# Loading q and k in runs of four tokens instead of two in a fused attention and SiLU kernel

## The chip, the core and the metric

The kernel runs on one core of a Trainium2 chip. The core has a matrix engine (TensorE, PE in the profile), a vector engine (VectorE, DVE), an activation engine (ScalarE, ACT), a general engine (GpSimd, POOL) and a queue engine (SyncE, SP) that here only issues transfers. Sixteen DMA engines move data between the device memory and the on-chip memory; each engine of the core works through its own instruction list in order and waits on semaphores for what others produce. The metric is the time of one execution in microseconds; lower is better.

## The reference

Eight batches with eight heads of attention over 576 tokens of 64 dimensions, with a decay made from the gates `f`, then a two-layer network with a SiLU on all 4,608 tokens:

```python
scores = scale * np.matmul(q, k.transpose(0, 1, 3, 2))
log_f = np.log(np.clip(f, 0.0001, 1.0))
cum = np.cumsum(log_f, axis=-1)
decay = cum[:, :, :, None] - cum[:, :, None, :]
scores = np.where(causal, -1000000000.0, scores + decay)
attn = softmax(scores)                  # over the last axis
x = (attn @ v) as [B * S, H * D]        # 4608 x 512
h = x @ w_in                            # 512 -> 2048
out = (h * sigmoid(h)) @ w_out          # 2048 -> 512
```

## The kernel before

**Pairs and tiles.** The 64 heads are worked in 16 groups of four (n = 0 to 15, two to a batch; below also called pairs, since q and k of a group share a tile). A group's q and k lie in one staging tile `stg` (two buffers): partition 32 j + t belongs to head j of the group and to token t of every run of tokens. `load_qk` issues one DMA for each head and tensor. Its access pattern takes the sequence in blocks of R x T tokens (T = 32): partition t gets R tokens that follow one another, so one contiguous piece has R x 64 floats. With R = 2 a piece has 512 bytes, a block has 64 tokens, and the 576 tokens are G = 9 blocks.

**From load to product.** `cast_qk` (mostly on GpSimd) turns fp32 in `stg` into bf16 in `raw`. `transposes` runs one VectorE transpose of 32 x 32 blocks over `raw` and writes `qkT`, in which a token is a column; because a partition holds R neighbouring tokens, neighbouring values of a transposed row go to columns R apart. TensorE then forms scores (`chunk`, line 350), ScalarE takes the exponential (line 360), GpSimd masks the diagonal blocks (line 387) and scales v by the decay (line 263), TensorE multiplies by v (line 429), and VectorE writes the normalised result to `xT` (line 457). The network follows on blocks of 512 tokens: `m1_chunk` (matrix product line 482, tanh line 490, gate line 493) and `m2_part` (product line 516, copy line 526, store line 527).

**The order.** Nothing is scheduled by a planner. The string `ORDER` lists the steps, each step adds its instructions to the engines' lists, and each engine follows its own list. The steps that the change and the prediction speak of:

- `G n.i` (lines 109 and 562): load the second part of group n's q (i = 0) or k (i = 1) on SyncE's queue, for n = 0 and 1 alone. The first part, blocks 0 to GA - 1 (256 tokens), is loaded ahead of the list. `L n.i`: the whole tensor, for n from 2.
- `y`, `c`, `C`: the casts of the first part, second part and the whole (line 136). `z`, `t`, `T`: the transposes of the same (line 279).
- `I i`, `O i`: a quarter of the first or second weight, issued by GpSimd on the software queue with a cast on the way (lines 190 and 199). `W`, `V`: load and scale a piece of v (lines 144 and 263).
- `S n.c`, `s i`: scores. `H`: half of a network step for the first 512 tokens, `A`: a whole one, `B`: a quarter of the second product.

On GpSimd the beginning of the list is: c0.0, c0.1, I0, two pieces of v, I1, one piece of v, c1.0, c1.1, I2, I3, C2.1, C2.0, O2. On SyncE it is: first parts, two pieces of v, G0.0, G0.1, two pieces of v, G1.1, G1.0, L2.1, a piece of v, L2.0, and on. Each DMA on the hardware queues waits on a semaphore for the one issued eight places before it.

Of the kernel before, what the change touches and what calls it, by code (L numbers as in the profile page):

```python
# [52 lines left out]
def kernel(  # L53
# [10 lines left out]
    nc = tc.nc  # L64

    B, H, S, D = q.shape
# [5 lines left out]
    QH = 4  # L72
# [3 lines left out]
    ST = S - SM  # L76
    NM = SM // P
    T = 32
    R = 2
    G = S // (R * T)  # L80
    E = R * D
    assert D == 64 and S == 576 and DM == H * D and H == QB * QH
    scale = 1.0 / float(D) ** 0.5
# [19 lines left out]
    vst: dict[int, list] = {}  # L103


    def qk_tile(n):
        return qkp.tile([P, 2, S * D // T], BF16, name="raw", tag="raw")

    def load_qk(n, i, engs, g0=0, g1=G, heads=(0, 2, 1, 3)):
        b, g = divmod(n, QB)  # L110
        direct = engs == (nc.gpsimd,)
        where = raw if direct else stg
        if n not in where:
            if direct:
                where[n] = qk_tile(n)
            else:
                where[n] = stage.tile([P, 2, S * D // T], FP32, name="stg", tag="stg", bufs=2)
        src = (q, k)[i]
        for j in heads:
            engs[j * len(engs) // QH].dma_start(  # L120
                out=where[n][j * T : (j + 1) * T, i, g0 * E : g1 * E].rearrange(
                    "p (g e) -> p g e", e=E
                ),
                in_=src[b, QH * g + j, g0 * R * T : g1 * R * T, :].rearrange(
                    "(g t c) d -> t g (c d)", t=T, c=R
                ),
            )

    def cast_qk(n, i, g0=0, g1=G, eng=nc.gpsimd):
        if n not in raw:  # L130
            raw[n] = qk_tile(n)
        r = slice(g0 * E, g1 * E)
        if eng is nc.scalar:
            eng.copy(out=raw[n][:, i, r], in_=stg[n][:, i, r])
        else:
            eng.tensor_copy(out=raw[n][:, i, r], in_=stg[n][:, i, r])  # L136
# [9 lines left out]
            in_=v[b, :, c * P : min(S, (c + 1) * P), :].rearrange("h p d -> p h d"),  # L146
        )

    GA = 4
    both = (nc.sync, nc.scalar)  # L150
    f_sb = setup.tile([BH, S], FP32, name="f_sb")
    nc.sync.dma_start(out=f_sb[:, :], in_=f.rearrange("b h s -> (b h) s"))
    for i in (1, 0):
        load_qk(0, i, both, 0, GA)
    load_qk(1, 0, (nc.sync,), 0, GA)
    nc.scalar.preload_act_table_set("natural_log_exp_and_others")
    for c in range(2):
# [10 lines left out]
        out=neg[:, :],  # L168
        in_=neg[:, :],
# [11 lines left out]
    for t in vps:  # L181
        nc.gpsimd.memset(t[0:ST, NM, :, :, :], 0.0)
    load_qk(1, 1, (nc.gpsimd,), 0, GA)

    WQ = 4
# [83 lines left out]

    def transposes(n, i, g0=0, g1=G):  # L270
        if n not in qkT:
            t = qktp.tile([P, 4 * S], BF16, name="qkT", tag="qkT")

            w = (0, GA * R * T, S) if n < QB else (0, S)
            qkT[n] = {
                w0: t[:, 4 * w0 : 4 * w1].rearrange("p (i x c) -> p i x c", i=2, x=2)
                for w0, w1 in zip(w, w[1:])
            }
        nc.vector.transpose(  # L279
            out=qkT[n][g0 * R * T][:, i, :, :].rearrange(  # L280
                "p x (g t c) -> p g c x t", t=T, c=R
            ),
            in_=raw[n][:, i, g0 * E : g1 * E].rearrange(
                "p (g c x e) -> p g c x e", c=R, x=2, e=T
            ),
        )

    def qk_cols(n, r, i, x, c0, w):
        o = max(o for o in qkT[n] if o <= c0)
# [262 lines left out]
    def nums(n):  # L552
# [5 lines left out]
        "u": decay_sum,  # L558
        "w": decay_weights,
        "y": lambda n, i: cast_qk(n, i, 0, GA, start_cast.get((n, i), nc.gpsimd)),  # L560
        "z": lambda n, i: transposes(n, i, 0, GA),
        "G": lambda n, i: load_qk(n, i, (nc.sync,), GA, G),
        "f": lambda n: products([(n, None)], 0, HB, "log"),
# [4 lines left out]
        "o": lambda i: gate(w_out_bf[0:1, (i + 1) * NFC // WQ - 1, 0:1], WQ + i),  # L568
        "L": lambda n, i: load_qk(n, i, (nc.sync,)),
        "c": lambda n, i: cast_qk(n, i, GA, G),  # L570
        "t": lambda n, i: transposes(n, i, GA, G),
        "C": cast_qk,
        "T": transposes,
        "W": load_v,
        "V": convert_v,
# [51 lines left out]
```

## Time and profile before

| what | value |
|---|---|
| runs | 353.04 and 351.63 us, median 352.34 |
| the profiled execution | 352.01 us, of which the span is 350.3 |
| PE busy | 323.5 us, 92% of the span |
| DVE busy | 222.8 us, 64% |
| ACT busy | 209.4 us, 60% |
| POOL busy | 129.1 us, 37% |
| DMA packets | 86416, 42.54 MB; 41128 of them under 512 B |
| DMA issues for q and k on SyncE | 136, median 0.45 us each |
| transposes of q and k on VectorE | 36, 46.4 us busy |

The span runs from the first to the last instruction; the execution's own time also has what lies around it. The busy share is a mean over the whole span. The page also cuts the span into 40 slices and gives each engine's busy share there in tenths (9 is 90% or more), and follows a chain of waits backward from the last instruction: at each step to what released it. TensorE's granted clock is full in nearly all of it (0.998).

### The profile page before, as it was taken

The numbers are of one execution on the slowest core, as the hardware profiler recorded it, in microseconds if no ns is written. First come the engines' busy times: TensorE is split into PE (matmuls) and PEld (weight loads), VectorE is DVE, ScalarE is ACT, GpSimd is POOL, SyncE is SP. The second block draws the span as 40 slices with busy tenths as digits, with TensorE's granted clock in tenths as the row PEclk, the third lists the DMA queues.
The fourth block names the chain that finished last, engine by engine and source line by source line (L and its number), as shares of the span: only waits on it lengthen the run. The fifth ranks groups of instructions, "written<-read, shape, count | busy, mean of one in ns | idle before, by whom it ended". The sixth has DMA issues, their size and how long they took to land.

```text
span 350.3 us, 8957 instructions
## 1 busy us (share of the span) xinstructions
PE 323.5 (92%) x3739; PEld 165.6 (47%) x3782; DVE 222.8 (64%) x297; ACT 209.4 (60%) x298; POOL 129.1 (37%) x172
## 2 busy tenths in 40 slices
PE   1667789999999999999999999999999999999996
PEld 1454554544455445444554455454445444444444
DVE  4466875688958696679867677679566834334310
ACT  3585796469854984599539855766574344444421
POOL 7771828628484362245543654322150000000000
PEclk9999999999999999999999999999999999999999
DMA  7999999898679803951299142223100000010102
GB/s 169 201 219 221 217 213 197 245 232 190 152 164 233 190 3 109 251 140 31 63 241 225 32 123 80 60 62 92 47 30 32 32 30 33 31 60 31 61 30 90
DMA packets 86416, 42.54 MB, mean 121 GB/s; under 512 B 41128, under 2 KB 81832, under 8 KB 86376
## 3 DMA queue, kind: packets, MB, share of 16 engines
q1 hardware_dynamic: 80936, 37.39, 43.7%
q0 software_dynamic: 4864, 4.33, 8.0%
q8 instruction: 29, 0.48, 0.6%
q10 hardware_dynamic: 576, 0.26, 0.3%
q14 instruction: 11, 0.09, 0.1%
HBM read 36.85 MB, written 9.44 MB: 132 GB/s over the span
## 4 chain that ended last, share of the span: by engine, by line
PE 79%; DMA 8%; ACT 4%; DVE 3%; issue 3%; POOL 2%; SPq 1%; ACTq 0%; POOLq 0%
PE po L516 34%; PE hp L482 30%; PE ps L429 9%; PE sc L350 6%; DMA w_in_bf<-in_moe_w_in_dram 3%; ACT u L360 2%; DMA stg<-in_k_dram 2%; DVE gt L493 2%; DMA vf<-in_v_dram 1%; ACT th L490 1%; POOL w_in_bf L190 1%; DMA f_sb<-in_f_dram 1%; POOL vp L263 1%; SPq L120 0%; POOL raw L136 0%
## 5 line engine op out<-in xcount | busy, mean ns | idle before, releaser
L493 DVE SCALAR_TENSOR_TENSOR gt<-th,hp 128x512 bf16<-128x512 bf16 (+1 forms) x160 | 96.1, 627 | 74.7 <-ACT th L490 74.0
L482 PE MATMUL hp<-xT,w_in_bf 128*128 128x512 bf16 (+1 forms) x622 | 135.7, 358 | 4.0 <-DMA w_in_bf<-in_moe_w_in_dram 3.0
L516 PE MATMUL po<-w_out_bf,gt 128*128 128x512 bf16 (+1 forms) x567 | 130.8, 373 | 3.1 <-issue 2.7
L490 ACT ACTIVATE th<-hp 128x512 bf16<-128x512 f32 (+1 forms) x160 | 83.8, 560 | 39.8 <-PE hp L482 37.6
L360 ACT ACTIVATE u<-sc 128x2048 bf16<-128x2048 f32 (+7 forms) x64 | 95.0, 1503 | 20.7 <-PE sc L350 20.6
L482 PEld LDWEIGHTS <-w_in_bf 128*128 128x128 bf16 x640 | 59.4, 98 | 66.4 <-issue 5.6
L516 PEld LDWEIGHTS <-gt 128*128 128x128 bf16 x592 | 55.3, 98 | 63.8 <-issue 2.8
L387 POOL TENSOR_SCALAR_AFFINE_SELECT u<-u 128x512 bf16<-128x512 bf16 (+1 forms) x70 | 40.0, 591 | 86.8 <-ACT u L360 86.3
L468 DVE RECIPROCAL rec<-rec 128x144 f32<-128x144 f32 x56 | 55.6, 1023 | 3.8 <-ACT rec L448 3.8
L279 DVE STREAM_TRANSPOSE qkT<-raw 128x1152 bf16<-128x1152 bf16 (+2 forms) x36 | 46.4, 1308 | 6.0 <-POOL raw L136 5.9
L263 POOL TENSOR_TENSOR vp<-vf,w_bf 128x512 bf16<-128x512 f32 (+1 forms) x40 | 41.4, 1041 | 18.3 <-DMA vf<-in_v_dram 17.4
L136 POOL CAST raw<-stg 128x1152 bf16<-128x1152 f32 (+2 forms) x34 | 36.2, 1075 | 28.4 <-DMA stg<-in_q_dram 24.2
L526 ACT ACTIVATE osb<-po 128x512 f32<-128x512 f32 (+1 forms) x37 | 21.7, 588 | 29.8 <-PE po L516 28.7
L350 PE MATMUL sc<-qkT 32*128 32x64 bf16 (+7 forms) x1064 | 32.4, 249 | 4.9 <-ACT u L360 2.9
L448 ACT ACTIVATE rec<-ps 128x192 f32<-128x192 f32 (+1 forms) x28 | 10.0, 408 | 43.4 <-DVE xT L457 43.1
L457 DVE TENSOR_TENSOR xT<-ps,rec 128x512 bf16<-128x512 f32 (+1 forms) x28 | 19.9, 753 | 16.2 <-PE ps L429 16.0
L350 PEld LDWEIGHTS <-qkT 32*128 32x128 bf16 x1064 | 17.6, 95 | 25.3 <-issue 20.3
L429 PEld LDWEIGHTS <-vp 128*32 128x32 bf16 x960 | 20.4, 98 | 3.9 <-issue 1.0
L429 PE MATMUL ps<-u,vp 128*32 128x320 bf16 (+4 forms) x784 | 21.6, 261 | 0.1
L429 PEld LDWEIGHTS <-w_bf 128*32 128x32 bf16 x480 | 9.2, 96 | 11.9 <-issue 8.1
L429 PE MATMUL ps<-u,w_bf 128*32 128x192 bf16 (+2 forms) x392 | 12.2, 263 | 0.1
L251 PE MATMUL wps<-ident_f,wexp 64*128 64x64 f32 x5 | 0.8, 316 | 7.6 <-ACT wexp L244 7.6
(37 smaller groups left out, 47.5 us busy)
## 6 DMA issues: line engine op xcount, KB each, us to landing
out_dram<-osb SPq DMA_DIRECT2D x35, 256.0 KB, 2.4
vf<-in_v_dram SPq DMA_DIRECT2D x32, 256.0 KB, 4.3
stg<-in_k_dram SPq DMA_DIRECT2D x56, 144.0 KB, 4.4
stg<-in_q_dram SPq DMA_DIRECT2D x56, 144.0 KB, 4.0
w_in_bf<-in_moe_w_in_dram POOLq DMA_DIRECT2D x8, 256.0 KB, 7.9
w_out_bf<-in_moe_w_out_dram POOLq DMA_DIRECT2D x4, 512.0 KB, 10.5
vf<-in_v_dram SPq DMA_DIRECT2D x8, 128.0 KB, 4.6
stg<-in_q_dram SPq DMA_DIRECT2D x8, 80.0 KB, 4.8
```

The source lines that it names most:

```text
L136: eng.tensor_copy(out=raw[n][:, i, r], in_=stg[n][:, i, r])
L263: nc.gpsimd.tensor_tensor(out=vp[r, c, :, :, :], in0=vst[b][c][r, :, :].rearrange("p h (r x) -> p h x r", x=2), in1=w_bf[r, c, b * H : (b ...
L279: nc.vector.transpose(out=qkT[n][g0 * R * T][:, i, :, :].rearrange("p x (g t c) -> p g c x t", t=T, c=R), in_=raw[n][:, i, g0 * E : g1 * E ...
L350: nc.tensor.matmul(sc[:, j, o : o + w], lhsT=qk_cols(n, r, 1, x, k_off(kb), P), rhs=qk_cols(n, r, 0, x, q0, w), start=(x == 0 and not unde ...
L360: nc.scalar.activation(out=us[n][:, :, c0:c1], in_=sc[:, :, at : at + c1 - c0], func=ACT.Exp, scale=scale,)
L387: nc.gpsimd.affine_select(out=x, in_=x, pattern=[[0, QH], [1, w]], compare_op=ALU.is_ge, fill=0.0, base=0 if kb < NM else ST, channel_mult ...
L429: nc.tensor.matmul(ps[32 * j : 32 * j + 32, o0 + q0 - e0 : o0 + q1 - e0], lhsT=w, rhs=us[n][:, j, o : o + q1 - q0], start=(kb == 0), stop= ...
L468: nc.vector.reciprocal(out=recs[n][:, r], in_=recs[n][:, r])
L482: nc.tensor.matmul(hp[:, 0 : hi - lo], lhsT=w_in_bf[:, cc, fc * P : (fc + 1) * P], rhs=xT[:, cc, t0 + lo : t0 + hi], start=(cc == 0), stop ...
L490: nc.scalar.activation(out=th[:, 0 : hi - lo], in_=hp[:, 0 : hi - lo], func=ACT.Tanh, scale=0.5)
L493: nc.vector.scalar_tensor_tensor(out=gt[:, fc, lo:hi], in0=th[:, 0 : hi - lo], scalar=1.0, in1=hp[:, 0 : hi - lo], op0=ALU.add, op1=ALU.mult,)
L516: nc.tensor.matmul(po[:, 0 : c1 - c0], lhsT=gt[:, fc, tb * P : (tb + 1) * P], rhs=w_out_bf[:, fc, c0:c1], start=(fc == 0), stop=(fc == NFC ...
```

## The change

R goes from 2 to 4, so a contiguous piece has four tokens or 1 KB, and a block 128 tokens. 576 tokens are four such blocks and 64 tokens more; this rest keeps the old form of two tokens (512 bytes) a partition. G counts it as a fifth block, and the new function `runs` splits a stretch of blocks into its main part and, if it reaches the end, the rest. `load_qk` issues one DMA for each of these parts, and `transposes` one transpose, so that a load or transpose of a whole sequence has two instructions where it had one. In the main part neighbouring values of a transposed row are written 4 columns apart, 8 bytes in bf16, instead of 2 columns, 4 bytes. GA becomes 2 blocks, which is 256 tokens as before. The casts keep their number; the columns of `raw` come in another order that the transposes undo. The list of steps is the same.

```diff
--- before.py
+++ after.py
@@ -76,8 +76,8 @@
     ST = S - SM
     NM = SM // P
     T = 32
-    R = 2
-    G = S // (R * T)
+    R = 4
+    G = S // (R * T) + 1
     E = R * D
     assert D == 64 and S == 576 and DM == H * D and H == QB * QH
     scale = 1.0 / float(D) ** 0.5
@@ -103,8 +103,13 @@
     vst: dict[int, list] = {}
 
 
+
     def qk_tile(n):
         return qkp.tile([P, 2, S * D // T], BF16, name="raw", tag="raw")
+
+    def runs(g0, g1):
+        main = [(R, g0, min(g1, G - 1))] if g0 < G - 1 else []
+        return main + ([(ST // T, G - 1, G)] if g1 == G else [])
 
     def load_qk(n, i, engs, g0=0, g1=G, heads=(0, 2, 1, 3)):
         b, g = divmod(n, QB)
@@ -117,19 +122,21 @@
                 where[n] = stage.tile([P, 2, S * D // T], FP32, name="stg", tag="stg", bufs=2)
         src = (q, k)[i]
         for j in heads:
-            engs[j * len(engs) // QH].dma_start(
-                out=where[n][j * T : (j + 1) * T, i, g0 * E : g1 * E].rearrange(
-                    "p (g e) -> p g e", e=E
-                ),
-                in_=src[b, QH * g + j, g0 * R * T : g1 * R * T, :].rearrange(
-                    "(g t c) d -> t g (c d)", t=T, c=R
-                ),
-            )
+            for r, ga, gb in runs(g0, g1):
+                t0 = ga * R * T
+                engs[j * len(engs) // QH].dma_start(
+                    out=where[n][
+                        j * T : (j + 1) * T, i, ga * E : ga * E + (gb - ga) * r * D
+                    ].rearrange("p (g e) -> p g e", e=r * D),
+                    in_=src[b, QH * g + j, t0 : t0 + (gb - ga) * r * T, :].rearrange(
+                        "(g t c) d -> t g (c d)", t=T, c=r
+                    ),
+                )
 
     def cast_qk(n, i, g0=0, g1=G, eng=nc.gpsimd):
         if n not in raw:
             raw[n] = qk_tile(n)
-        r = slice(g0 * E, g1 * E)
+        r = slice(g0 * E, min(g1 * E, S * D // T))
         if eng is nc.scalar:
             eng.copy(out=raw[n][:, i, r], in_=stg[n][:, i, r])
         else:
@@ -146,7 +153,7 @@
             in_=v[b, :, c * P : min(S, (c + 1) * P), :].rearrange("h p d -> p h d"),
         )
 
-    GA = 4
+    GA = 2
     both = (nc.sync, nc.scalar)
     f_sb = setup.tile([BH, S], FP32, name="f_sb")
     nc.sync.dma_start(out=f_sb[:, :], in_=f.rearrange("b h s -> (b h) s"))
@@ -276,14 +283,16 @@
                 w0: t[:, 4 * w0 : 4 * w1].rearrange("p (i x c) -> p i x c", i=2, x=2)
                 for w0, w1 in zip(w, w[1:])
             }
-        nc.vector.transpose(
-            out=qkT[n][g0 * R * T][:, i, :, :].rearrange(
-                "p x (g t c) -> p g c x t", t=T, c=R
-            ),
-            in_=raw[n][:, i, g0 * E : g1 * E].rearrange(
-                "p (g c x e) -> p g c x e", c=R, x=2, e=T
-            ),
-        )
+        for r, ga, gb in runs(g0, g1):
+            c0 = (ga - g0) * R * T
+            nc.vector.transpose(
+                out=qkT[n][g0 * R * T][:, i, :, c0 : c0 + (gb - ga) * r * T].rearrange(
+                    "p x (g t c) -> p g c x t", t=T, c=r
+                ),
+                in_=raw[n][:, i, ga * E : ga * E + (gb - ga) * r * D].rearrange(
+                    "p (g c x e) -> p g c x e", c=r, x=2, e=T
+                ),
+            )
 
     def qk_cols(n, r, i, x, c0, w):
         o = max(o for o in qkT[n] if o <= c0)
```

## The prediction

> **What bounds the kernel now.** I read the page first: the span, then the rows of the tenths.
>
> ```profile
> span 350.3 us, 8957 instructions
> ...
> PE   1667789999999999999999999999999999999996
> ...
> DMA  7999999898679803951299142223100000010102
> ```
>
> A slice is 8.76 us. From the eighth slice on TensorE is full, and there is little left to win there: the busy times by stretch give PE 41.07 us of the first 60, then 58.58 of 60, 127.43 of 130 and 96.48 of 100. So 18.9 us are idle in the first 60 us and only 7.5 in all that follows. In those first 60 us the DMA row is full. A faster load can therefore pay only there, and only where a landing is waited for. The chain of waits for 10 to 46 us (start, length, what) shows where that is:
>
> ```profile
> 10.97 1.97 DMA stg<-in_k_dram
> ...
> 13.08 0.72 POOL raw L136
> 13.80 1.43 POOL w_in_bf L190 x2
> ...
> 17.17 5.84 DMA stg<-in_k_dram
> ...
> 23.04 0.72 POOL raw L136
> 23.75 2.12 POOL w_in_bf L190 x3
> 25.88 11.61 DMA w_in_bf<-in_moe_w_in_dram
> ...
> 37.53 0.41 PE hp L482 x2
> ```
>
> GpSimd works in order. It waits for the second halves of q and k (steps c0, then c1), casts them, and only then issues the quarters of the first weight (I0, I1, later I2, I3). TensorE waits for the last quarter until 37.5. So a late k delays the weights, not only the scores. What feeds that chain is SyncE's queue (start, length, issues; steps G0.0, G0.1, V, G1.1, G1.0):
>
> ```profile
> 6.49 2.81 SPq L120 DMA_DIRECT2D stg<-in_q_dram  x4
> 9.34 1.94 SPq L120 DMA_DIRECT2D stg<-in_k_dram  x4
> 11.32 1.06 SPq L144 DMA_DIRECT2D vf<-in_v_dram  x2
> 12.43 2.49 SPq L120 DMA_DIRECT2D stg<-in_k_dram  x4
> 14.97 2.07 SPq L120 DMA_DIRECT2D stg<-in_q_dram  x4
> ```
>
> It issues without a pause. The steady pace is 0.48 us an issue (1.94 / 4), whatever is moved. An 80 KB load of 160 packets takes 160 x 27 ns / 16 engines = 0.27 us of transfer (27 ns is the median of the trace's 512-byte packets). In this stage the q and k loads are bound by their **issue**, not by bytes. The instruction lists also show that each hardware load waits for the one eight places before it, so eight are under way at most.
>
> **What the Trainium skill says.** "DMA: Bandwidth & Descriptors", section "Why small descriptors are slow (HBM only)": each packet carries a fixed overhead. The trace agrees: medians of 27 ns for 512 B, 46 for 1 KB and 84 for 2 KB make about 8 ns fixed plus 0.037 ns a byte. The same page, "Queues, rings and completion order": each engine takes turns between queues, packet by packet. The trace agrees here too; from 45 to 50 us the software queue (weights) and the hardware queue (q, k, v) had nearly as many packets:
>
> ```profile
> q0 software_dynamic: 713, 0.71, 85.0%
> q1 hardware_dynamic: 700, 0.34, 34.0%
> ```
>
> The same page, "Issuing engines are not separate DMA queues", calls the time to initiate a DMA usually small beside the DMA. Here it is not: 0.48 us against 0.27. "SBUF — State Buffer", under "Door 1: The DMA port swizzle", gives 16-byte lines that need two hits each for full bandwidth; a write every 8 bytes has just two. The trace of before has only the 4-byte stride.
>
> **The change part by part.**
>
> *Fewer packets.* A head's q or k goes from 288 packets of 512 B to 128 of 1 KB and 32 of 512 B: 7.78 us of engine time become 128 x 46 + 32 x 27 ns = 6.75. The second DMA adds 16 completion packets of about 10 ns. That leaves 0.86 us, or 0.054 us over 16 engines; the 40 heads' tensors of pairs 0 to 4 that are loaded by about 50 us make 2.1 us. It helps only if the DMA engines are what is waited for. In the first loads (256 tokens, no tail) an engine's share falls from 8 x 27 to 4 x 46 ns, some 0.4 us over the dozen loads, of which I take -0.2 us on the path (0 to -0.4).
>
> *Twice the issues.* Every load that reaches the end of the sequence gets a tail DMA: 28 whole loads and 4 second halves, four heads each, 128 more on SyncE. A tail has two dimensions; the nearest row is the store of the output, 0.36 us, or 0.45 if it costs what a load costs, plus 0.05 to the next. The 16 tails of G0 and G1 then cost 6.6 to 8.0 us in a stretch that has no pause. Against that stand some 0.7 us of back-pressure (issues of 1.25 and 1.04 us in the groups at 6.49 and 12.43) and a shorter way to landing: the last G1.0 load was issued at 16.56 and landed at 22.3, 5.8 us later, because it took turns with weights. With a backlog gone I take 3 us. So it lands at 16.56 + 6.6 - 0.7 + 3.0 = 25.5, **3.2 us later** (bounds: 2 us earlier if the turns with weights rule, 5 later). A cast now waits for eight landings instead of four; the extra waits are entries of about 0.02 us each on GpSimd's queue. Everything queued behind the waiting casts on GpSimd shifts with them: V0, I0 to I3, then C2.
>
> *What of it reaches TensorE.* From 24.47 (scores after t1) to 37.53 there are 13.06 us, of which 0.51 + 1.59 + 0.92 = 3.02 are waits for w_in. Started 3.2 later, TensorE would be at the same step at 24.47 + 3.2 + 10.04 = 37.7. The quarters I2 and I3 are issued at 26.9 instead of 23.7. They are 64 packets an engine of 96 ns, 6.1 us alone; they took 13.8 us from first issue to last landing. With fewer bytes of q and k in flight I estimate 12, landing at 38.9. The path shifts by **+1.4 us** (0.2 if TensorE's own work decides, 3.5 if q and k keep the weights back as before). After that ScalarE and TensorE set the pace, and nothing takes it back.
>
> *Later loads.* From 60 to 91 us and from 98 to 118 SyncE issues almost without rest; 32 and 16 tails lie there. Cover: it idled 91 to 98 and 118 to 134 (waiting to store), and casts mostly run after their data. If the cover is gone, the v load behind the wait of 7.8 us on GpSimd at 119.4 comes some 1 to 2 us later, then cast C9.0 and transpose T9.0 (124.56), and behind it on VectorE the gates that TensorE waits for. I take +0.5 (0 to 1.5).
>
> *Transposes.* The durations by shape (busy, mean ns):
>
> ```profile
> L279 DVE STREAM_TRANSPOSE qkT<-raw 128x1152 bf16<-128x1152 bf16 x28 | 40.4, 1454 | 3.4 <-POOL raw L136 3.4
> L279 DVE STREAM_TRANSPOSE qkT<-raw 128x640 bf16<-128x640 bf16 x4 | 3.3, 881 | 2.6 <-POOL raw L136 2.6
> L279 DVE STREAM_TRANSPOSE qkT<-raw 128x512 bf16<-128x512 bf16 x4 | 2.7, 718 | 0.1
> ```
>
> Two of the large ones in a row take 2.78 us, two of the small 1.33, so 1.39 and 0.67 each: 1.13 ns an element and 0.09 fixed. Splitting 1152 into 1024 and 128 adds 0.09 us, 32 times: 2.8 us on VectorE, which has 76% of 120 to 250 us busy. I put +0.4 on the path (0 to 1.5) and the 8-byte stride at nothing, by the skill's line rule; its upper end is rival two.
>
> Sum: 1.4 - 0.2 + 0.5 + 0.4 = **+2.1 us**. The profiled execution took 352.01, so 354.1 there; it lies 0.33 under the median of the runs, 352.34, so **354.4** as a median.
>
> **Rivals.** *One, the bytes win.* If the turns between queues rule (the landing lag of 5.8 us speaks for it), wider packets bring q and k 73% more bytes in the same time (1024 B in 96 + 46 ns, against 512 in 96 + 27), the casts come earlier and the saved 2.1 us reach the end: 350.2. Against it: the steady 0.48 us pace with 0.27 us of transfer, and weights that then come later. *Two, the stride is dear, and it is slower.* If an 8-byte stride halves the rate, the large transposes take 2.3 us instead of 1.25. From 60 to 250 us there are 22 of them, +23 us on 145.0 busy of 190, 88%. With two fifths of it reaching TensorE (my choice: TensorE is otherwise full and VectorE works in order ahead of it), 9.4 us; with the sum above, 364. It decides (over 7 us in all) from about 1.8 us for a 128x1024 transpose. Nothing in the trace shows it; the full rate at 4 bytes speaks against it. *Three, SyncE falls behind for good* between 60 and 118 us: the 48 tails cost 20 us of issue, and 4 us beyond the cover delay q, k and v for two pairs and add to my sum: 358.4. *Four, the change doesn't take place:* the built lists show 128 more loads and runs of 256 elements, so I give this nothing.
>
> **How the numbers follow.** My forecast (own range 352.5 to 358.9, its lower and upper terms) gets 0.63, rival one 0.22, rival two 0.10, rival three 0.05. The range from 350.5 to 359 leaves out the better half of rival one and all of rival two. A measurement here tells about 2%, 7 us, from no change. Faster by that needs more than three times the saving of rival one: 0.02. Slower: rival two, half of three, and a thin edge of mine: 0.13. Within: 0.85.
>
> **What would show it.** Right: the last G1 load is issued near 23 and landed near 25.5, the second c1 cast starts there, and the wait of TensorE for w_in ends near 38.9; DMA less full from 8 to 27 us. Wrong: the c1 cast before 22.4 (rival one), a 128x1024 transpose over 1.8 us (rival two), or SyncE's stores after 98 us running late (rival three). A tail issue well under 0.36 us would halve my shift.

## The result, and the profile after

The changed kernel takes 371.78 us (two runs, 371.25 and 372.32) against 352.34: a ratio of 1.0552, interval 1.0441 to 1.0663. It is slower by 19.4 us, where 2.1 had been forecast, and lies above the range. The profiled execution has a span of 369.3 us, 19.0 more than before.

The first lines of the page of the changed kernel (busy microseconds, then the tenths of 40 slices, here of 9.23 us each):

```profile
PE 328.8 (89%) x3739; PEld 168.1 (46%) x3782; DVE 256.7 (70%) x329; ACT 209.9 (57%) x298; POOL 129.4 (35%) x172
...
PE   1565864999899999999999999999999999999996
...
PEclk9996997899999999999999999999999999999999
DMA  7597899657666773176224573312311011000202
```

TensorE is over 80% busy in the fifth slice, dips again in the sixth and seventh, and is full only from the eighth on. Its idle time is 369.3 - 328.8 = 40.5 us, against 350.3 - 323.5 = 26.8, and its busy time is 5.3 us longer for the same 3739 recorded matmuls. So 13.7 of the 19.0 us are new idle time and 5.3 are slower work. The granted clock shows where the slower work is:

```profile
23.00:29.60 6.60, 2.68 (x72) 1.00 0.78 150
29.60:36.40 6.80, 4.14 (x56) 0.50 0.83 151
...
53.00:60.30 7.30, 3.76 (x48) 1.00 1.19 230
60.30:67.10 6.80, 4.39 (x92) 0.50 0.87 205
```

These are stretches of the changed kernel: length, PE busy, granted clock, DMA share, GB/s. Twice TensorE is busy for about half of some 7 us, and in the 6.8 us after that it gets half the clock. If work at half the clock takes twice as long, half of 4.14 + 4.39 = 4.3 of the 5.3 us comes from there (an estimate). "TensorE: Matmul & The Clock Gate", section "HAM oscillation — how this bites in real kernels", of the Trainium skill describes this: waiting on DMA long enough lets the clock fall for what follows. The trace agrees: the clock falls both times within one of TensorE's two longest waits after 10 us, 5.0 and 4.6 us, both for q and k that came late. This loss is a consequence of lateness, not its cause.

The lateness is all there early. The by-stretch sums give PE 33.10 us of the first 60 (41.07 before) and 54.11 of the next 60 (58.58); after 120 us hardly anything more is lost (126.5 of 130, against 127.4). The chain of waits from 5 to 76 us stays on SyncE's queue until 73 us; before, it left SyncE's transfers for GpSimd at 23 us and reached TensorE at 37.5 (start, length, what):

```profile
16.31 5.75 DMA stg<-in_k_dram
22.07 5.40 DMA stg<-in_q_dram
...
36.69 7.74 DMA stg<-in_q_dram
...
51.80 6.87 DMA stg<-in_k_dram
58.69 6.43 DMA stg<-in_k_dram
...
68.87 3.81 DMA vf<-in_v_dram
72.74 0.64 POOL u L396
73.38 1.10 POOL raw L143
74.50 2.48 DVE qkT L288
```

The first five pieces named DMA are landings that the chain runs through because SyncE could not issue before them: each is a transfer eight places back. The last, of v, is waited for on GpSimd. SyncE's own list (start, time for all the issues of the row, how many) and what it waited for up to 75 us (total, times, longest) say the same:

```profile
6.47 4.96 SPq L127 DMA_DIRECT2D stg<-in_q_dram  x8
11.47 3.70 SPq L127 DMA_DIRECT2D stg<-in_k_dram  x8
15.21 1.05 SPq L151 DMA_DIRECT2D vf<-in_v_dram  x2
16.31 5.35 SPq L127 DMA_DIRECT2D stg<-in_k_dram  x8
22.07 5.13 SPq L127 DMA_DIRECT2D stg<-in_q_dram  x8
...
33.23 13.21 SPq L127 DMA_DIRECT2D stg<-in_q_dram  x16
46.49 13.75 SPq L127 DMA_DIRECT2D stg<-in_k_dram  x16
```

```profile
SPq L127 <- DMA stg<-in_k_dram: 7.7, 10, 1.5
```

Eight issues without a wait take 3.70 us, 0.47 from one to the next. Beside the weights (16 to 27 us) eight take over 5, and in the two long rows 16 take over 13, 0.84 each. A 16 KB tail costs SyncE as much as a main transfer (0.42 us and 0.05 to the next) and holds one of the eight places until it lands: three tails issued from 18.4 to 21.3 us landed 4.4 to 5.5 us later, a main transfer of 64 KB among them 4.7 us later. From 30 to 66 us SyncE issues 46 transfers, 0.78 us apart, where it issued 29, 1.24 us apart, before: more transfers, fewer bytes.

What TensorE waits for most between 20 and 80 us has changed from w_in (the first line, before) to q and k (the second, after):

```profile
PE hp L482 <- DMA w_in_bf<-in_moe_w_in_dram: 3.0, 3, 1.6
```

```profile
PE sc L359 <- DVE qkT L288: 11.6, 4, 5.0
```

And the transposes, shape by shape (busy, mean ns):

```profile
L288 DVE STREAM_TRANSPOSE qkT<-raw 128x1024 bf16<-128x1024 bf16 x28 | 68.5, 2447 | 7.0 <-POOL raw L143 7.0
L288 DVE STREAM_TRANSPOSE qkT<-raw 128x128 bf16<-128x128 bf16 x32 | 10.9, 340 | 0.1
L288 DVE STREAM_TRANSPOSE qkT<-raw 128x512 bf16<-128x512 bf16 x8 | 10.1, 1312 | 7.0 <-POOL raw L143 6.9
```

128x1024 takes 2.45 us where 128x1152 took 1.45; 512 takes 1.31 where it took 0.72. The 8-byte stride is dear. Two causes are thus open side by side: later loads and slower transposes.

### The profile page after: what moved, and what is told of

Same layout as the page of the kernel before. It is cut to its first block, busy times and chain, and to the rows that moved or that the text cites. A ratio compares the mean times of both kernels' runs of the same rounds, so it can differ in the third digit from the quotient of the medians.

```text
span 369.3 us, 9160 instructions
## 1 busy us (share of the span) xinstructions
PE 328.8 (89%) x3739; PEld 168.1 (46%) x3782; DVE 256.7 (70%) x329; ACT 209.9 (57%) x298; POOL 129.4 (35%) x172
## 4 chain that ended last, share of the span: by engine, by line
PE 63%; DMA 11%; DVE 9%; SPq 9%; ACT 3%; issue 3%; POOL 1%; ACTq 0%; POOLq 0%
PE po L525 30%; PE hp L491 22%; SPq L127 7%; PE ps L438 7%; DVE qkT L288 5%; DMA stg<-in_k_dram 5%; DMA stg<-in_q_dram 4%; PE sc L359 4%; DVE gt L502 2%; ACT u L369 2%; SPq L151 1%; DMA vf<-in_v_dram 1%; ACT th L499 1%; DVE xT L466 1%; DMA f_sb<-in_f_dram 1%
## 5 line engine op out<-in xcount | busy, mean ns | idle before, releaser
L491 PE MATMUL hp<-xT,w_in_bf 128*128 128x512 bf16 (+1 forms) x622 | 137.3, 361 | 4.5 <-DVE gt L502 2.7
L502 DVE SCALAR_TENSOR_TENSOR gt<-th,hp 128x512 bf16<-128x512 bf16 (+1 forms) x160 | 95.0, 623 | 62.6 <-ACT th L499 62.3
L288 DVE STREAM_TRANSPOSE qkT<-raw 128x1024 bf16<-128x1024 bf16 (+1 forms) x68 | 83.6, 1322 | 14.1 <-POOL raw L143 13.9
L491 PEld LDWEIGHTS <-w_in_bf 128*128 128x128 bf16 x640 | 60.6, 99 | 67.7 <-issue 9.4
L270 POOL TENSOR_TENSOR vp<-vf,w_bf 128x512 bf16<-128x512 f32 (+1 forms) x40 | 41.4, 1042 | 22.0 <-DMA vf<-in_v_dram 20.6
L359 PE MATMUL sc<-qkT 32*128 32x64 bf16 (+7 forms) x1064 | 34.6, 257 | 14.9 <-DVE qkT L288 12.3
L535 ACT ACTIVATE osb<-po 128x512 f32<-128x512 f32 (+1 forms) x37 | 21.8, 588 | 29.1 <-PE po L525 28.0
L438 PE MATMUL pn<-u,vp 128*32 128x64 bf16 (+2 forms) x176 | 5.6, 284 | 3.1 <-POOL vp L270 3.1
## 6 DMA issues: line engine op xcount, KB each, us to landing
w_out_bf<-in_moe_w_out_dram POOLq DMA_DIRECT2D x4, 512.0 KB, 10.2
```

What stands on the lines that cost most here:

```text
L270: nc.gpsimd.tensor_tensor(out=vp[r, c, :, :, :], in0=vst[b][c][r, :, :].rearrange("p h (r x) -> p h x r", x=2), in1=w_bf[r, c, b * H : (b ...
L288: nc.vector.transpose(out=qkT[n][g0 * R * T][:, i, :, c0 : c0 + (gb - ga) * r * T].rearrange("p x (g t c) -> p g c x t", t=T, c=r), in_=ra ...
L359: nc.tensor.matmul(sc[:, j, o : o + w], lhsT=qk_cols(n, r, 1, x, k_off(kb), P), rhs=qk_cols(n, r, 0, x, q0, w), start=(x == 0 and not unde ...
L438: nc.tensor.matmul(ps[32 * j : 32 * j + 32, o0 + q0 - e0 : o0 + q1 - e0], lhsT=w, rhs=us[n][:, j, o : o + q1 - q0], start=(kb == 0), stop= ...
L491: nc.tensor.matmul(hp[:, 0 : hi - lo], lhsT=w_in_bf[:, cc, fc * P : (fc + 1) * P], rhs=xT[:, cc, t0 + lo : t0 + hi], start=(cc == 0), stop ...
L502: nc.vector.scalar_tensor_tensor(out=gt[:, fc, lo:hi], in0=th[:, 0 : hi - lo], scalar=1.0, in1=hp[:, 0 : hi - lo], op0=ALU.add, op1=ALU.mult,)
```

## The experiments

All times are medians. Ratios are to the kernel before, run beside it on the same chip (352.1 to 353.1 us). A difference in us is one of medians; the ratio that goes with the interval can differ a little from the quotient of the medians (`issues_alone`: 1.0536 against 1.0559).

### Loads alone, stride alone, split alone

`loads_alone` keeps the loads of the changed kernel and transposes each load at once with the 4-byte stride, so tokens come in another order. `stride_alone` keeps the loads of before and splits and strides the transposes as the change does; `split_alone` only splits them (1024 and 128 elements).

```diff
+        for r, ta, tb in ((4, o, min(g1 * R * T, SM)), (2, SM, g1 * R * T)):
+            if ta < tb:
+                nc.vector.transpose(
...
+                        "p x (g t c) -> p g c x t", t=T, c=r
```

(`split_alone` has 2 in place of the 4.)

> The loads of the change (1 KB runs and a tail DMA each) with one transpose a load at the old 4-byte stride, so that the tokens of q and k come to wrong columns and the scores are of other tokens. Theory L (twice the issues on SyncE, eight transfers under way at most): most of the loss is here, 10 to 15 us over before, 362 to 367; the second c1 cast near 30 us as in the changed kernel. Theory S (the stride): 2 to 4 us over before, 354 to 356.

> The loads of before with the transposes of the change (two instructions a load, the larger at an 8-byte stride), so that the scores are of other tokens. Theory L: 4 to 8 us over before, 356 to 360, with transposes of 2.4 us as in the changed kernel. Theory S: 14 us or more over before, 366 and up.

> The loads of before; each transpose split in two instructions (1024 and 128 elements) at the 4-byte stride. Both theories: within 1 us of before, since it adds some 3 to 6 us to VectorE in the whole. If it costs over 3 us, the number of instructions and not the stride is what slows the transposes.

| run | time us | ratio | interval |
|---|---|---|---|
| loads_alone | 370.49 | 1.0492 | 1.0429 to 1.0554 |
| stride_alone | 358.91 | 1.0142 | 1.0104 to 1.0181 |
| split_alone | 352.89 | 0.9993 | 0.9974 to 1.0013 |

The loads alone bring 17.4 us, the stride alone 5.8 (358.91 - 353.09), the split nothing. Together they bring 19.4 where the sum is 23.2. The interval of the change, 15.5 to 23.4 us, reaches the sum, so it isn't shown that the two overlap; it would be natural if part of the slow transposes cost nothing where q and k come late anyway. In `stride_alone` VectorE has 20.7 us more work between 60 and 250 us (165.7 against 145.0), and 5.8 us reach the end: 28% of it, if the slower transposes before 60 us cost nothing.

### What a write stride costs

`strides` transposes whole loads of 1152 elements with different distances between neighbouring writes. Groups 0, 1, 6, 7, 13 and 14 keep 4 bytes; of the others two have 2, 6, 12, 18 and 36 bytes each, and their tokens are permuted.

```diff
+            nc.vector.transpose(**view(2))
...
+            nc.vector.transpose(**view(1))
...
+            nc.vector.transpose(**view(3))
...
+            nc.vector.transpose(**view(6))
...
+            nc.vector.transpose(**view(9))
...
+            nc.vector.transpose(**view(18))
```

> The loads of before; for the groups from the third on, the 1152-element transpose writes at a stride of 2, 4, 6, 12, 18 or 36 bytes, one stride a group, each on a line of its own, so that the scores of most groups are of other tokens. If the rate follows how many writes fall in a 16-byte line: 2 and 4 bytes alike at 1.4 us, 6 bytes between, 8 and over near 2.6 us or more, growing until one write a line. If it only tells 4 bytes or less from more: 6, 12, 18 and 36 bytes all alike near 2.6 us.

The groups of the run by line, the dearest first (busy, mean ns), for 18, 36, 12, 6, 4 and 2 bytes in turn:

```profile
L297 DVE STREAM_TRANSPOSE qkT<-raw 128x1152 bf16<-128x1152 bf16 x4 | 21.0, 5338 | 1.0 <-POOL raw L136 1.0
L299 DVE STREAM_TRANSPOSE qkT<-raw 128x1152 bf16<-128x1152 bf16 x4 | 20.2, 5148 | 0.0
...
L295 DVE STREAM_TRANSPOSE qkT<-raw 128x1152 bf16<-128x1152 bf16 x4 | 16.1, 4022 | 0.0
...
L293 DVE STREAM_TRANSPOSE qkT<-raw 128x1152 bf16<-128x1152 bf16 x4 | 8.4, 2101 | 0.2 <-POOL raw L136 0.2
...
L289 DVE STREAM_TRANSPOSE qkT<-raw 128x1152 bf16<-128x1152 bf16 x4 | 5.6, 1428 | 0.0
L291 DVE STREAM_TRANSPOSE qkT<-raw 128x1152 bf16<-128x1152 bf16 x4 | 5.4, 1357 | 0.0
```

Divided by 1152: 1.18 ns an element at 2 bytes, 1.24 at 4, 1.82 at 6, 3.49 at 12, then flat at about 4.5; at 8 bytes the changed kernel has 2447 / 1024 = 2.39. From 4 to 12 bytes it grows by 0.28 ns a byte. That is close to what a fixed price of about 4.5 ns for each 16-byte line touched would give, with a floor near 1.2 ns: an element pays its share of a line, a quarter of it at 4 bytes, half at 8 (2.25 by this rule, 2.39 measured). Two writes a line are not enough for the full rate; four are. The run as a whole took 384.45 us in its one execution.

### Issues alone, two queues, wide packets

`issues_alone` keeps runs of two tokens and the transposes of before, and only issues each load that reaches the end as two transfers of 512 and 64 tokens. `two_queues` is the same with the tails of pairs 0 and 1 on ScalarE's queue. `wide_alone` keeps the number of transfers and makes each partition's piece one run (2, 2.5 or 4.5 KB), so tokens come in another order.

```diff
+            for ga, gb in ((g0, min(g1, G - 1)), (G - 1, g1)):
+                if ga < gb:
+                    eng = engs[j * len(engs) // QH]
...
+                    if ga == G - 1 and n < QB:
+                        eng = nc.scalar
```

(The last two lines in `two_queues` alone.) For `wide_alone`:

```diff
-                    "(g t c) d -> t g (c d)", t=T, c=R
+                    "(t c) d -> t (c d)", c=w
```

> The 512-byte runs and transposes of before; only each load that reaches the end of the sequence is issued as two DMAs (512 and 64 tokens). Theory L: at least four fifths of what loads_alone loses, or more, since the packets stay narrow: 362 to 368. If the loss came of the 1 KB runs themselves: no more than 2 us over before.

> issues_alone, with the tails of the first two groups (16 DMAs) issued from ScalarE's queue instead of SyncE's. If the time of an issue is what delays the loads, the second c1 cast comes 5 us or more earlier than the 29 us of issues_alone. If the limit of eight transfers under way is, which both queues share, it comes at most 2 us earlier, and ScalarE waits in addition.

> As many DMAs as before and the transposes of before, but each partition gets one contiguous run (2, 2.5 or 4.5 KB), so that the tokens of q and k come in another order and the scores are of other tokens. It asks what wider packets are worth without a further issue. Rival one of the prediction (the bytes win): 2 to 4 us under before. Theory L: also at most that, 349 to 352, since 512 and 1 KB packets differ by 3 us between issues_alone and loads_alone.

| run | time us | ratio | interval | c1 casts, us |
|---|---|---|---|---|
| issues_alone | 372.84 | 1.0536 | 1.0491 to 1.0582 | 29.5 |
| two_queues | 365.90 (one execution) | – | – | 27.5 |
| wide_alone | 357.48 | 1.0132 | 1.0103 to 1.0160 | 22.7 |

(The last column is the start of the two c1 casts on GpSimd in the profiled execution: 22.4 before, 30.1 in the changed kernel.) The doubled issues alone bring 19.8 us, no less than all the loads of the change (17.4); that its wider packets give some of it back is possible, but the intervals overlap. Taking the early tails off SyncE's own list brings c1 forward by only 2.1 us of 7.2. The eight places are counted over both hardware queues: in `two_queues` SyncE's issue at 14.43 us waits for a tail that ScalarE had issued at 11.73. The last early tail is issued 5.2 us sooner (21.9 instead of 27.1 us), yet the casts gain 2.1: the tail issued just before it, beside I1's weights, takes 5.6 us to landing, where the last of `issues_alone` took 2.3. ScalarE issues its tails between its exponentials, so this run doesn't price the time to issue by itself; that it is the lesser part for the cast is a reading and not a measurement. The end comes 6.9 us earlier, more than the cast explains: the loads of pair 2 gain too (C2.0 at 41.7 us instead of 45.5), and one execution doesn't divide the rest. What SyncE waits for in `issues_alone` up to 75 us is places:

```profile
SPq L123 <- DMA stg<-in_k_dram: 9.3, 9, 2.5
SPq L123 <- DMA vf<-in_v_dram: 4.6, 1, 4.6
```

`wide_alone` is the test of rival one, with the issue count held. Its casts of pair 2 do come earlier (C2.0 at 30.6 us against 36.2), those of c1 don't, and it is slower. The chain shows where:

```profile
23.38 0.72 POOL raw L135
...
26.23 16.43 DMA w_in_bf<-in_moe_w_in_dram
42.67 0.05 issue
42.71 0.41 PE hp L481 x2
```

The wait for the last quarter of w_in starts at 26.2 us, as before (25.9), and lasts 16.4 us instead of 11.6. From 26 to 38 us the software queue (weights) moved 0.85 MB where it had moved 1.05, the hardware queue (q, k, v) 2.07 where it had moved 1.64. That fits turns by packet: a wider packet of q or k takes longer for its turn, and what it gains the weights lose. One rival stands untested: with C2.0 earlier, the first quarter of w_out is issued at 31.7 us instead of 37.3, on the queue in which w_in is still under way.

### Where the doubled issues cost

The same split, in `issues_alone`'s form, for a part of the loads only: pairs 0 and 1 (`early_tails`), pairs 2 to 4 (`mid_tails`), pairs 5 to 15 (`late_tails`). `merged_tails` splits all loads, but loads the tails of four heads in one transfer of 64 KB.

```diff
+            for ga, gb in ((g0, min(g1, G - 1)), (G - 1, g1)) if n < QB else ((g0, g1),):
```

```diff
...
+        if g1 == G:
+            engs[0].dma_start(
+                out=where[n][:, i, (G - 1) * E :],
+                in_=src[b, QH * g : QH * (g + 1), (G - 1) * R * T :, :].rearrange(
+                    "h (t c) d -> h t (c d)", c=R
+                ),
+            )
```

(The condition is `QB <= n < 5` in `mid_tails` and `n >= 5` in `late_tails`.)

> Runs of two tokens as before; only the second halves of q and k of pairs 0 and 1 are loaded in two transfers (16 more, all issued before 30 us). Places theory (eight transfers under way, each 16 KB tail holds a place for its whole landing time): the second c1 cast starts near 29, as with all loads split (29.5), against 22.4 before; TensorE has the last w_in some 5 us later, and nothing after gives it back: 357 to 359. Rival (a delay this early is taken up by TensorE's later waits): c1 late all the same, but the end within 1.5 us of before: 353 to 354.5.

> Only the whole loads of pairs 2 to 4 are made in two transfers (24 more, issued from about 17 to 66 us beside the weights). Places theory: the c1 cast up to 2 us later at most, but q and k of pairs 2 to 4 land 6 to 9 us later, TensorE waits for qkT near 55 to 75 us, and the end is at 360 to 363. Rival (early delay is what counts): 353 to 355.

> Only the whole loads of pairs 5 to 15 are made in two transfers (88 more, two thirds of all). Places theory: with the weights in, places come free within 2 us and SyncE has rests, so the end is at 353 to 355. Rival (each added issue costs the same, 19.8 us over 128): 88 of them cost 13.6 us: 366 to 367.

> Runs of two tokens; the last 64 tokens of the four heads of a load go in one transfer of 64 KB over all partitions instead of four of 16 KB (32 more instead of 128). Places or issue time, both counted per transfer: a quarter of the 19.8 us of all split loads, 357 to 359, with the c1 cast near 24 to 25. Rival (the split as such costs, since the cast waits for a second kind of landing or for the tail's packets, whatever their number): 365 to 373, c1 near 29.

| run | more transfers | time us | ratio | interval | us more, per transfer |
|---|---|---|---|---|---|
| early_tails | 16 | 359.77 | 1.0212 | 1.0171 to 1.0254 | 7.3, 0.46 |
| mid_tails | 24 | 358.35 | 1.0171 | 1.0140 to 1.0203 | 5.9, 0.25 |
| late_tails | 88 | 356.85 | 1.0122 | 1.0095 to 1.0149 | 4.4, 0.05 |
| merged_tails | 32 | 358.86 | 1.0157 | 1.0106 to 1.0208 | 6.4, 0.20 |

The three parts add to 17.6 of the 19.8 us. What a transfer costs depends on the stage by a factor of nine: 40 of the 128 bring three quarters. The casts show how the first two parts add. C2.0 and the two casts of q and k behind it came at 36.2, 40.0 and 42.5 us before. In `early_tails` they are 8.0, 8.0 and 8.1 us later, in `mid_tails` 1.0, 2.9 and 7.5, and in the changed kernel 8.9, 9.6 and 16.5. So the early tails shift all that follows by one amount, and the loads of pairs 2 to 4 build up a delay of their own. `mid_tails` and `late_tails` missed their expected times, one below and one above, and `early_tails` is a little above; late is neither free nor as dear as early. In `late_tails` SyncE's cover is what is eaten: up to 140 us from 75 it waits to store only this long, 25.2 us before, and TensorE is busy 26.0 us of 110 to 140, against 29.4 before:

```profile
SPq L530 <- ACT osb L529: 10.6, 3, 10.0
```

`merged_tails` ended where the count of transfers had it (358.9 us), but not in the way that the count says, so that hit is luck. With a quarter of the added transfers c1 should have started near 24.5; it started at 29.1, hardly before `early_tails` (30.1). The queues between 18 and 22 us (packets, MB, share) show what happened there:

```profile
q0 software_dynamic: 453, 0.45, 84.0%
q1 hardware_dynamic: 193, 0.09, 9.5%
```

In the same four microseconds of the kernel before:

```profile
q0 software_dynamic: 378, 0.36, 60.9%
q1 hardware_dynamic: 1087, 0.51, 48.8%
```

The q loads of pair 1 were not in the queue when the weights began: they are issued from 18.9 us on, and I0 at 16.8. Two more runs took pair 0 and pair 1 separately (`n == 0` and `n == 1` as the condition), each with 8 more transfers, to see whether it is this order that counts.

> Only the second halves of q and k of pair 0 are loaded in two transfers (8 more, issued by about 15 us); pair 1 and all later loads as before. Order theory (what counts is that the loads of pair 1 slip behind the weight transfers I0 and I1 and then take turns with them): the second c0 cast near 15 to 16.5 instead of 13.1, I0 and I1 later by as much, the last load of pair 1 issued near 21, the first c1 cast at 27 to 29.5 and the end at 357.5 to 360, nearly all of what 16 more transfers cost (30.1 and 359.8). Additive theory (each transfer the same): half of it, c1 near 26.2, end near 356.

> Only the second halves of q and k of pair 1 are loaded in two transfers (8 more, issued between about 12 and 21 us). Order theory: the c0 casts and I0, I1 are where they were (12.3, 13.8, 17.2), the last load of pair 1 is issued near 20.5, after I1, and lands with I1's weights, which were all in at 26.3: c1 at 26 to 27.5, end at 355 to 357.5. Additive theory: c1 near 26.2, end near 356 like the run with pair 0 alone; the two together, 7.3 us, then are the sum of the two alone. If instead pair 1 alone costs less than 1.5 us, the early delay lies with the c0 casts alone.

| run | last load of pair 1 issued | I1 issued | c1 casts | time us, ratio, interval |
|---|---|---|---|---|
| before | 16.6 | 17.2 | 22.4 | – |
| early_n1 (8 more) | 22.7 | 17.8 | 26.9 | 355.48, 1.0084, 1.0053 to 1.0115 |
| early_n0 (8 more) | 21.2 | 20.7 | 27.7 | 356.12, 1.0115, 1.0089 to 1.0140 |
| merged_tails (4 more) | 21.1 | 20.3 | 29.1 | see above |
| early_tails (16 more) | 27.0 | 20.6 | 30.1 | see above |

(The issue and cast times are those of the one profiled execution of each.) For the casts the runs speak for the order theory: 8 transfers move c1 by 4.5 or 5.4 us, 16 by 7.7, and 4 by 6.7. Its ranges were 26 to 27.5 us for `early_n1` (26.9) and 27 to 29.5 for `early_n0` (27.7); the additive theory had 26.2 for both. In the kernel before the last load of pair 1 is issued ahead of I1; in each of the others it is behind, and then it shares its way with I1's weights. Two runs that add no transfer to pairs 0 and 1 show the same. In `split_alone` that load is issued at 17.72 us, 0.12 ahead of I1, lands 6.0 us later, and c1 starts at 23.8. In `three_tokens`, below, it is issued at 17.31, 0.04 behind I1, lands 8.0 us later, and c1 starts at 25.4. The load that was issued sooner lands later.

For the end, though, the two parts simply add (3.4 + 4.0 = 7.4 against 7.3), and `early_n0` ended below the time that the order theory gave it. Why the end follows the sum and the casts don't is open. Why 4 transfers in `merged_tails` delay c1 more than 8 in `early_n0` and `early_n1` is not settled either: its last transfer is a tail of 64 KB, as large as each of the four before it, where the others end on 16 or 80 KB, but no run separates size from place. No run changed the number of places or when the weights are issued, so the wait for a place and the landing beside weights aren't priced apart.

### Three tokens, no tail

192 runs of three tokens fill 576 without a rest. `three_tokens` loads pairs from 2 on in runs of 768 bytes, one transfer a head as before, and writes at a 6-byte stride.

```diff
+        R, G0 = (3, 6) if n >= QB else (2, 9)
+        E = R * D
```

> From the third group on, runs of three tokens (768 bytes, six blocks, no rest), so one DMA a head as before, 192 packets instead of 288, and transposes at a 6-byte stride in one instruction. It computes what the reference does. If a 6-byte stride is nearly free, 1 to 3 us under before; if it costs what 8 bytes cost, 4 to 6 us over.

355.13 us, ratio 1.0057, interval 1.0019 to 1.0095. The large transposes take 2.09 us (1.45 before), the c1 casts start at 25.4. So wider runs without a second transfer but with a 6-byte stride gain nothing together; this run doesn't say what each does. None of the versions tried is faster than the kernel before.

## Why the prediction was wrong

**The bound: right, with a gap.** TensorE idle early, SyncE's issues behind the casts, the casts ahead of the weight issues: all of that is seen again. TensorE is even fuller later than the 7.5 us of idle time after the first 60 say. The trace before has 3739 matmul records; `early_n0` and `early_n1` have 3782, as many as there are weight loads, and no wait of TensorE from 60 to 350 us where the trace before shows 17 of at most 0.2 us, 2.7 in all. So those are most likely missing records. The gap: the text reads the 0.48 us pace as the limit and names the eight places in one sentence without a price for what the new transfers hold.

**"So it lands at 16.56 + 6.6 - 0.7 + 3.0 = 25.5": the term of back-pressure failed.** The last load of pair 1 was issued at 26.8 us and landed at 30.1. The lag of 3.0 was right for this load (3.3), though for those issued beside I0 and I1, at 18.4 to 21.3 us, it was 4.4 to 5.5. The 16 tails at 0.47 us are 7.5, within the bounds given. What failed is "- 0.7": the waits for a free place did not shrink, they grew. The last load is issued 26.8 - 16.56 = 10.2 us later, 2.7 more than the tails' own 7.5, and a 16 KB transfer was seen to hold its place as long as a 64 KB one. The c1 casts came 7.8 us late instead of 3.2, above the stated bound of 5, and the last w_in at 43.3 instead of the forecast 38.9. The 12 us that I2 and I3 were given from issue to landing were right (31.5 to 43.3). `early_tails` prices this term at 7.3 us, against 1.4.

**No term for the loads of pairs 2 to 4.** After w_in the sum has nothing until 60 us; "ScalarE and TensorE set the pace, and nothing takes it back" holds for the part before, but the loads issued from 17 to 66 us make a delay of their own: 7.5 us at the third cast from C2.0 on, and by itself this part costs 5.9 us at the end (`mid_tails`), where the sum had nothing. Of the two stretches of half clock `early_tails` has the first (30.0 to 36.7 us); the profiled execution of `mid_tails`, the quickest of its four, has none, so which part brings the second isn't settled.

**Later loads: "+0.5 (0 to 1.5)".** They cost 4.4 us alone (`late_tails`), what rival three gave them, since the waiting to store that was named as cover shrinks from 25.2 to 10.6 us. How much of it shows in the changed kernel, where everything is late already, was not measured.

**"The 8-byte stride at nothing, by the skill's line rule": wrong.** "SBUF — State Buffer", "Door 1: The DMA port swizzle", says that two hits a 16-byte line suffice. For this instruction the measurement decides: 2.39 ns an element at 8 bytes against 1.24 at 4. Rival two had the mechanism and its duration (2.3 us; measured 2.45). Its price of 9.4 was 5.8 alone and about 2 on top of late loads (19.4 - 17.4, from ratios whose intervals overlap). It was given a chance of 0.10 because the trace had only one stride, and one stride can't speak for or against a threshold.

**The split of the transposes: right in size.** +0.4 us was forecast; `split_alone` measured -0.2, with an interval of -0.9 to +0.5. (Its transposes take 51.1 us in all where they took 46.4, so 4.7 us more on VectorE and not 2.8, and none of it reaches the end.)

**Rival one falls.** Wider packets do bring q and k of pair 2 sooner, and the weights come later (`wide_alone`, +4.5 us). The forecast had named that objection.

**The range** was built from bounds on terms that shared one belief: that an added transfer costs its issue time alone, and that rests of SyncE and of the casts cover most of it. When the belief failed, all of them failed to the same side.

## What to carry to other kernels

Price a transfer by the place it holds from issue to landing and by where in the order it lands, not only by its bytes and issue time: halving the packet overhead with a second small transfer loses, if the number of transfers under way is capped. Ask of each load which large transfer it is issued ahead of, for slipping behind it can cost more than the slip (here 8.0 us to landing instead of 6.0). Before writing at a wider stride, look for the same instruction at two strides; if there is none, keep both prices in the range with real weight.

## What the runs showed of the hardware

- A bf16 VectorE transpose takes 1.18 ns an element with 2 bytes between neighbouring writes and 1.24 with 4; then the price rises by about 0.28 ns an element and byte to 3.49 at 12 bytes, and is 4.63 and 4.47 at 18 and 36.
- A 16 KB load costs SyncE the same 0.42 us as one of 128 KB, and takes 2.2 (q) or 2.7 us (k) at the median from issue to landing, where 128 KB takes 2.4 or 2.8: eight times the bytes add 0.1 to 0.2 us.
- With wider packets in one queue the other moved less (0.85 MB instead of 1.05 from 26 to 38 us in `wide_alone`), and the last w_in came at 42.7 us instead of 37.5.
- A load issued 0.04 us behind a weight transfer took 8.0 us to landing, one issued 0.12 us ahead of it 6.0 (`three_tokens`, `split_alone`).
- In the changed kernel 6.8 us of half clock follow stretches in which TensorE was busy for 41% and 52% of the time; one of 7 us at 55%, just before the first, kept the full clock. The share doesn't decide by itself, nor does one long wait: from 10 to 20 us TensorE was busy for 42% at full clock, and in `early_n0` 3.7 us of reduced clock (0.54 in the mean) follow 3.6 us at 48% with no wait over 1.5 us.
